# FNet and GEGLU layers on one core: the down projection of the last layer as seven block products that give y^T

## The chip, the cores and the metric

The kernel runs on one core of a Trainium2 chip. TensorE (PE) multiplies, VectorE (DVE) and ScalarE (ACT) work elementwise, GpSimd (POOL) and SyncE (SP) issue DMAs here; POOL also computes a few one-column values. The metric is the device time of one execution in microseconds (us). Three runs of the kernel before gave 1659.72, 1661.08 and 1661.01, median 1661.01.

## The reference

Four layers alternate, each as x + layer(layernorm(x)), all in float32. x is 2048 tokens by D = 512, F = 1792.

```
def _A_ref(x, dft_seq_re, dft_seq_im, dft_hid_re, dft_hid_im):
    a = jnp.einsum("bsd,ed->bse", x, dft_hid_re)
    b = jnp.einsum("bsd,ed->bse", x, dft_hid_im)
    return jnp.einsum("ts,bse->bte", dft_seq_re, a) - jnp.einsum("ts,bse->bte", dft_seq_im, b)
def _B_ref(x, w_gate, w_up, w_down):
    return (_gelu(x @ w_gate) * (x @ w_up)) @ w_down

x = x + _A_ref(_layernorm(x), ...)   # layer 0
x = x + _B_ref(_layernorm(x), ...)   # layer 1
x = x + _A_ref(_layernorm(x), ...)   # layer 2
x = x + _B_ref(_layernorm(x), ...)   # layer 3
```

## The kernel before

**Precision.** Every float32 operand of a product is split into two float32r tiles: ScalarE copies it to hi (line 126), VectorE computes lo = x - hi (line 127). A product of two split operands is three matmuls, hi by hi, hi by lo, lo by hi: `mm3`, lines 160 to 162. Each has a 128x128 stationary operand and a 128x512 moving one.

**Storage.** All working tiles of 128x512 come from `sb`, a list of NSLOT = 98 slots of SBUF that are taken from the front of a free list and put back at its end; accumulators come from `ps8`, the eight banks of PSUM. During part of a mix layer the tile `wide` (four slots' size) is lent to the list (`lend`, `reclaim`). The program is written in the Tile framework, which orders each engine's instructions at build time by a model of their readiness, so the order of the calls is a priority and not the order of execution.

**Mix layers (0 and 2).** The sequence DFT and the hidden DFT; the first is already done with seven block products instead of eight (Strassen-Winograd): `a11`, `a12`, `s2`, `s4` run over blocks b of 512 tokens, `hid_groups` follows.

**GEGLU layers (1 and 3).** `geglu(w, layer)` handles 1024 tokens at a time, w = 0 and 1, as two parts of 512 tokens. For n from 0 to 13 `up(n)` computes 256 columns' worth of gate (n even) or up (n odd) products, also as seven block products (S2, S1, A11 of n+1, S3, S4, A12 of n+1, A22; six matmuls each). ScalarE copies some of the sums out of PSUM (`copied`, line 155), VectorE adds others (line 151), ScalarE applies gelu (line 825), VectorE multiplies (line 839); the results are h[f, part], 128 columns of F by 512 tokens, transposed.

**The down projection before.** `down_steps(f, part)` takes the split w_down rows of f, already divided in DRAM (`wds`), and multiplies for each of four 128-token groups i: stationary is h[f, part] for these tokens, moving is w_down[f], 128x512; the sum over f = 0..13 gathers in `acc[part][i]`. `ready` splits h up to EARLY = 2 steps ahead. Eight steps of part 0 run between the products of `up` (from n = LAG = 6 on), the last six and the 14 of part 1 after the loop. `add_rows` adds x to the four sums (`x_add`, line 196) and POOL writes the rows (line 198). In the very last half, `last_downs` (TAIL = 4) orders the last four f by token group, so that each group of rows is added and written by SP while the next is multiplied.

**Queues.** `take` hands out operands in a fixed list, `items`; `load_next` issues their loads on SP (line 239) some items ahead (AHEAD, RAW, and NEAR for those that need no split, `whole`). Other work (norms, the blocks of the next half from `block_steps`, loads of divided gate and up weights by `piece_load`, line 815) is put into `queue`, and `step` runs one entry per product. `weight_steps(n)` loads gate and up weights in layer 1, forms S1 to S4, splits them and writes them to DRAM from POOL (lines 226 and 795). `terms_ahead`, `first_rows`, `second_rows` and `combine` prepare the next mix layer at the end of layer 1.

Of the kernel before, what the change touches and what calls it, by code (L numbers as in the profile page):

```python
# [14 lines left out]
P = 128  # L15
# [10 lines left out]
AHEAD = 5  # L26
RAW = 4
WARM = 16
LAG = 6
NEAR = 2  # L30
# [3 lines left out]
NSLOT = 98  # L34
FORE = {0: 4, 2: 2}
TAIL = 4
# [4 lines left out]
def fnet_geglu(ctx: ExitStack, tc: tile.TileContext, x_in, ws, wh, wgu, wdn, out):  # L41
# [33 lines left out]
    tpool = ctx.enter_context(tc.tile_pool(name="turned", bufs=1))  # L75
    slots = ctx.enter_context(tc.tile_pool(name="slots", bufs=1))
# [12 lines left out]
    class Slots:  # L89


        def __init__(self, pool, name, n):
            self.pool, self.name, self.free, self.held = pool, name, list(range(n)), {}
            self.least, self.lending = n, False
# [9 lines left out]
        def put(self, *tiles):  # L104
            for t in tiles:
                n = self.held.pop(id(t))[0]
                if isinstance(n, int) or self.lending:
                    self.free.append(n)

        def lend(self, tile):  # L110

            self.lending = True
            self.free = [(tile[:, i * 512:(i + 1) * 512],) for i in range(NT)] + self.free

        def reclaim(self):
            self.lending = False
            self.free = [n for n in self.free if isinstance(n, int)]
# [62 lines left out]
    def x_load(layer, i):  # L180
        t = sb.get()
        nc.sync.dma_start(t, rows(layer, i))
        return t
# [35 lines left out]
    wds = {f: dram.tile([P, 1024], F32, name=f"wd{f}") for f in range(NF)}  # L219

# [9 lines left out]
    stream = {"loaded": 0, "split": 0, "used": 0}  # L230
    raws, parts = {}, {}

    def load_next():
        n = stream["loaded"]
        dtype, addresses, _, _ = items[n]
        raws[n] = []
        for a in addresses:
            t = sb.get(dtype)
            stream["last"] = nc.sync.dma_start(t if dtype == F32 else f32(t), a)
            raws[n].append(t)  # L240
        stream["loaded"] += 1

    def split_next():
        n = stream["split"]
        while stream["loaded"] <= min(n + RAW, len(items) - 1):
            if stream["loaded"] > n + NEAR and items[stream["loaded"]][2] is whole:
                break
            load_next()
        parts[n] = items[n][2](*raws.pop(n))
        stream["split"] += 1  # L250

    def take():
        n = stream["used"]
        while stream["split"] <= min(n + AHEAD, len(items) - 1):
            need = items[stream["split"]][3]
            if need and need not in cs and stream["split"] > n:
                break
            if items[stream["split"]][2] is whole and stream["split"] > n + NEAR:
                break
            split_next()  # L260
        stream["used"] += 1
        return parts.pop(n)
# [93 lines left out]

    def mix_items(layer):
        def raw(make, *tiles):
            items.append((F32, tiles, make, None))

        for b, what in plan(layer):
            tiles = [[ws[(b * 2 + m) * NS + k] for k in range(NS)] for m in range(2)]
            (a11, a12), (a21, a22) = ((r[:NK], r[NK:]) for r in tiles)
            hold = b >= FORE[layer]
            if what == "A11":
                for k in range(NK):
                    raw(as_is if bare(layer, b, what) else make_a11(k) if hold else plain, a11[k])
            elif what == "A12":
                for t in a12:
                    raw(plain, t)  # L370
            elif what == "S2":
                for i, k in skewed(3):
                    if i == 0:
                        raw(make_s2(k), a21[k], a22[k], *(() if hold else (a11[k],)))
                    else:
                        raw(make_s1(k) if i == 1 else make_s3(k))
            elif what == "S4":
                for i, k in skewed(2):
                    if i == 0:
                        raw(make_s4(k), a12[k])  # L380
                    else:
                        raw(plain, a22[k])
            else:
                for m, c in what:
                    if layer == 0 and b == 0:
                        items.append((F32, (wh[m * ND + c],), make_hid_first(m, c), (m, c)))
                    else:
                        items.append((F32R, halves(whs[m, c]), make_hid(m, c), (m, c)))

    for layer in range(0, 4, 2):  # L390
        mix_items(layer)
        for w in range(NB // 2):
            for part in range(2):
                for f in range(NF):
                    if layer == w == part == 0:
                        items.append((F32, (wdn[f],), make_down_first(f), None))
                    else:
                        items.append((F32R, halves(wds[f]), whole, None))
# [87 lines left out]
    def second_rows(layer, k):  # L486
        second_norm(layer, k)
        second_parts(k)
# [32 lines left out]
    def block_steps(layer, w):  # L521
# [4 lines left out]
        def norm(i):  # L526

            def run():
# [5 lines left out]
                if n == 0:  # L534
                    assert all(isinstance(n, int) for n, _ in sb.held.values())
                    wide[part] = tpool.tile([P, NT * D], F32, name="wide")
# [66 lines left out]
    def mix(layer):  # L603
# [54 lines left out]
        def a12(b):  # L658
            side = [ps8.get() for _ in range(2)]
            for k in range(NK):  # L660
                six(side, "B21", k, k == 0, k == NK - 1)
# [17 lines left out]
        def s2(b):  # L679
            last, fore = b == NB - 1, b < FORE[layer]  # L680
            if b == 0:
                sb.lend(tpool.tile([P, NT * D], F32, name="wide"))
            if b == NB - 3:
                sb.reclaim()
# [77 lines left out]
    pieces = (("A11", "A12"), ("S2", "S3"), ("S1", "A22"), ("S4",))  # L762
# [4 lines left out]
    def weight_steps(n):  # L767
# [3 lines left out]
        def load():  # L771
# [4 lines left out]
            with tc.issue_after(stream["last"].ins):  # L776
                nc.sync.dma_start(src[0], wgu[n, :, :512])
                nc.sync.dma_start(v["A22"], wgu[n, :, 512:768])
                nc.sync.dma_start(v["A21"], wgu[n, :, 768:])
# [7 lines left out]
        def divide(i):  # L787
            def run():
                to = wblocks[n][:, i * 1024:min((i + 1) * 1024, 7 * 512)]
# [6 lines left out]
                piece_here(n, i, t)  # L796
# [3 lines left out]
        return load, [sums] + [divide(i) for i in range(len(pieces))]  # L800

# [26 lines left out]
    def geglu(w, layer):  # L828
# [71 lines left out]
        def up(n, down):  # L900
# [5 lines left out]
            u[n] = copied(chain[n])  # L906
            next(down, None)
# [35 lines left out]

        xrows = []
# [8 lines left out]
        def last_downs(tail):  # L953

            fs = range(NF - tail, NF)
            vs = [take() for _ in fs]
            for f in fs:
                ready(f, 1)
            for i in range(NT):
                ts = slice(i * P, (i + 1) * P)  # L960
                for f, v in zip(fs, vs):
                    hs = h[f, 1]
                    mm3(acc[1][i], (hs[0][:, ts], hs[1][:, ts]), v, f == 0, f == NF - 1)
                x_add(layer, (w * 2 + 1) * NT + i, xrows.pop(0), acc[1][i], engine=nc.sync)

        before_mix = w == 1 and layer < 3
        if before_mix:
            slow.extend((lambda k=k: terms_ahead(layer + 1, k, NK)) for k in range(NK))
        if w == 0:
            norms, others = block_steps(layer, 1)  # L970
            slow.extend(norms)
        first(0)
        second(0)
        for n in range(NF):
            up(n, down_steps(n - LAG, 0) if n >= LAG else iter(()))
        for bc in list(blocks):
            sb.put(*blocks.pop(bc))
        load_rows(0)
        if w == 0:
            while slow:  # L980
                slow.pop(0)()
            queue.extend(others)
        elif before_mix:
            queue.extend((lambda k=k: first_rows(layer + 1, k)) for k in range(NK))
            for k in range(NT):
                queue.append(lambda k=k: second_rows(layer + 1, k))
                queue.append(lambda k=k: combine(k))
            queue.extend((lambda k=k: combine_late(k)) for k in range(NT))
        for f in range(NF - LAG, NF):
            down(f, 0)  # L990
        add_rows(0)
        if w == 0:
            queue.extend((lambda n=n, i=i: piece_load(n, i)) for n in range(2) for i in range(len(pieces)))
        tail = TAIL if layer == 3 and w == 1 else 0
        for f in range(NF - tail):
            if f == NF - max(2, tail + 1):
                load_rows(1)
            down(f, 1)
            while len(queue) > 2 * (NF - 1 - f):
                step()  # L1000
        if tail:
            last_downs(tail)
        else:
            add_rows(1, before_mix)
        if before_mix:
            queue.extend((lambda k=k: second_rows(layer + 1, k)) for k in range(NT, NK))
            queue.extend((lambda k=k: combine(k)) for k in range(NT, NK))
            queue.extend((lambda k=k: combine_late(k)) for k in range(NT, NK))
# [85 lines left out]
```

## Time and profile before

| | |
|---|---|
| median of three runs | 1661.01 us |
| the profiled execution's own time | 1656.89 us |
| its span, first to last instruction | 1655.1 us |
| PE busy | 1637.7 us, 99% |
| DVE, ACT, POOL busy | 1027.5, 780.5, 188.9 us |
| granted TensorE clock, mean | 0.998 |
| moved by DMA | 399.99 MB |

Line numbers L... are those of the kernel before. A row of a group reads: line, engine, operation, out<-in by the program's names (s a slot, p a bank of PSUM), shapes, count, then busy time and mean duration of one, then how long the engine sat idle before them and what ended that. A row of stages reads: the stretch in us from the span's start, its length, then for each engine busy time and (number of instructions), the granted clock, the share of the 16 DMA engines' time and GB/s. Layer 3 starts at about 1233 us; its second half starts at about 1442 us.

### The profile page before, as it was taken

What the parts mean: (1) busy time and instruction counts of PE and PEld (TensorE: products, weight loads), DVE (VectorE), ACT (ScalarE), POOL (GpSimd) and SP (SyncE); (2) the same over time, 40 slices, a digit from 0 to 9 for tenths busy, and PEclk for the clock granted to TensorE, in tenths of its full rate; (3) what the DMA queues carried; (4) which work ended last, traced back from release to release, by engine and by line L of the source; (5) the groups of instructions that cost most, each with busy time, mean ns of one, the idle gap of its engine ahead of it and who ended that gap; (6) DMA issues with size and microseconds to landing.
All of it is one profiled execution on the core that took longest, in us unless ns stands there. A gap on an engine that the chain in (4) does not pass through costs nothing.

```text
span 1655.1 us, 22345 instructions
## 1 busy us (share of the span) xinstructions
PE 1637.7 (99%) x7168; PEld 1345.6 (81%) x7168; DVE 1027.5 (62%) x1756; ACT 780.5 (47%) x1496; POOL 188.9 (11%) x344
## 2 busy tenths in 40 slices
PE   9999998999999999999999999999999999999999
PEld 6878887877888888888878888888888888888887
DVE  8997777798776643334598776777944336233251
ACT  7743335545676524435584333664545435133330
POOL 3211001112544101000110000110010000000000
PEclk9999999999999999999999999999999999999999
DMA  9768677879976898566665767686798657956471
GB/s 364 235 217 278 209 241 250 288 274 321 355 271 240 284 367 275 174 183 213 233 216 185 221 210 230 206 269 227 214 340 296 198 164 243 374 171 191 148 240 51
DMA packets 218965, 399.99 MB, mean 242 GB/s; under 512 B 27232, under 2 KB 47200, under 8 KB 217824
## 3 DMA queue, kind: packets, MB, share of 16 engines
q1 hardware_dynamic: 200256, 333.02, 61.8%
q0 software_dynamic: 18592, 65.55, 10.5%
q8 instruction: 56, 0.92, 0.2%
q14 instruction: 61, 0.50, 0.1%
HBM read 331.87 MB, written 66.58 MB: 241 GB/s over the span
## 4 chain that ended last, share of the span: by engine, by line
PE 89%; DVE 4%; DMA 2%; ACT 2%; issue 1%; POOL 1%; SPq 0%; DVEq 0%; POOLq 0%; ACTq 0%
PE p L161 30%; PE p L160 29%; PE p L162 29%; DVE s L127 3%; DVE s L148 1%; DMA s<-x 1%; PE p L647 1%; ACT s L126 1%; DVE s L151 0%; ACT s L438 0%; DMA s<-ws 0%; DMA x<-s 0%; POOL rstd L432 0%; ACT s L440 0%; DMA s<-m_sum 0%
## 5 line engine op out<-in xcount | busy, mean ns | idle before, releaser
L161 PE MATMUL p<-s,s 128*128 128x512 f32 x2368 | 922.5, 390 | 6.9 <-DVE s L127 6.8
L162 PE MATMUL p<-s,s 128*128 128x512 f32 x2368 | 910.3, 390 | 0.0
L160 PE MATMUL p<-s,s 128*128 128x512 f32 x2368 | 902.0, 390 | 5.0 <-DVE s L151 3.9
L126 ACT ACTIVATE s<-s 128x512 fp32r<-128x512 f32 (+1 forms) x754 | 437.4, 616 | 448.2 <-DVE s L148 119.7
L127 DVE TENSOR_TENSOR s<-s,s 128x512 fp32r<-128x512 f32 (+1 forms) x754 | 484.8, 674 | 95.4 <-ACT s L126 62.4
L161 PEld LDWEIGHTS p<-s,s 128*128 128x128 f32 x2368 | 445.2, 188 | 103.7 <-DVE s L127 11.0
L160 PEld LDWEIGHTS p<-s,s 128*128 128x128 f32 x2368 | 445.0, 188 | 100.4 <-DVE s L151 3.6
L162 PEld LDWEIGHTS p<-s,s 128*128 128x128 f32 x2368 | 445.1, 188 | 93.7 <-DVE s L127 0.8
L151 DVE TENSOR_TENSOR s<-s,p 128x512 f32<-128x512 f32 x320 | 213.6, 683 | 349.1 <-PE p L162 283.9
L148 DVE TENSOR_TENSOR s<-s,s 128x512 f32<-128x512 f32 (+1 forms) x296 | 174.1, 604 | 50.3 <-DMA s<-ws 26.7
L155 ACT ACTIVATE s<-p 128x512 f32<-128x512 f32 x216 | 126.5, 592 | 151.6 <-PE p L162 148.7
L825 ACT ACTIVATE s<-s 128x512 f32<-128x512 f32 x112 | 70.4, 628 | 90.8 <-DVE s L151 89.6
L151 DVE TENSOR_TENSOR s<-s,s 128x512 f32<-128x512 f32 (+1 forms) x69 | 43.5, 633 | 51.8 <-DMA s<-ws 34.7
L198 POOL DMA_DIRECT2D x<-s x48 | 26.4, 551 | 357.0 <-DVE s L151 355.5
L441 POOL TENSOR_SCALAR rstd<-rstd 128x1 f32<-128x1 f32 x48 | 14.5, 301 | 455.4 <-ACT s L440 360.5
L438 ACT ACTIVATE s<-s 128x512 f32<-128x512 f32 x48 | 29.9, 623 | 65.7 <-DMA s<-x 53.8
L839 DVE TENSOR_TENSOR s<-s,s 128x512 f32<-128x512 f32 x84 | 57.8, 689 | 1.8
L226 POOL DMA_DIRECT2D wb<-s x84 | 45.8, 547 | 101.1 <-ACT s L126 69.6
L460 ACT ACTIVATE s<-s,shift,rstd 128x512 f32<-128x512 f32 x64 | 51.4, 808 | 9.8 <-DVE shift L433 6.0
L198 POOL DMA_DIRECT2D out<-s x12 | 6.5, 543 | 291.4 <-DVE s L151 288.4
L839 DVE TENSOR_TENSOR s<-s,p 128x512 f32<-128x512 f32 x28 | 19.2, 685 | 28.7 <-PE p L162 28.7
L440 ACT ACTIVATE s<-s,mean 128x512 f32<-128x512 f32 x48 | 34.3, 715 | 0.6
(47 smaller groups left out, 316.9 us busy)
## 6 DMA issues: line engine op xcount, KB each, us to landing
s<-ws SPq DMA_DIRECT2D x408, 256.0 KB, 4.1
s<-wb SPq DMA_DIRECT2D x294, 256.0 KB, 4.3
s<-wd SPq DMA_DIRECT2D x196, 256.0 KB, 4.7
s<-wh SPq DMA_DIRECT2D x118, 256.0 KB, 4.6
s<-x SPq DMA_DIRECT2D x102, 256.0 KB, 4.7
wb<-s POOLq DMA_DIRECT2D x98, 256.0 KB, 4.3
x<-s POOLq DMA_DIRECT2D x48, 256.0 KB, 4.7
s<-x SPq DMA_DIRECT2D x128, 64.0 KB, 3.4
```

The source lines that it names most:

```text
L126: nc.scalar.activation(hi, src, AF.Copy)
L127: nc.vector.tensor_tensor(lo, src, f32(hi), op=ALU.subtract)
L148: nc.vector.tensor_tensor(out, a, b, op=ALU.subtract)
L151: nc.vector.tensor_tensor(out, a, b, op=ALU.add)
L155: nc.scalar.activation(v, src, AF.Copy)
L160: nc.tensor.matmul(ps, ah, bh, start=start, stop=False, skip_group_check=True)
L161: nc.tensor.matmul(ps, ah, bl, start=False, stop=False, skip_group_check=True)
L162: nc.tensor.matmul(ps, al, bh, start=False, stop=stop, skip_group_check=True)
L226: nc.gpsimd.dma_start(a, f32(t))
L460: nc.scalar.activation(z, x, AF.Identity, bias=shift, scale=rstd)
L825: nc.scalar.activation(t, g, AF.Gelu_apprx_tanh)
L839: nc.vector.tensor_tensor(t, t, v, op=ALU.mult)
```

## The change

In layer 3, both halves (`SEVEN`), the products with w_down are computed transposed and by blocks. A pair k of F blocks (k = 0..6) and the two token parts make h a 2x2 block matrix; w_down's rows of the pair and the two halves of D make the other. Seven products per k, each with the weights' 128x128 pieces as the stationary operand and a combination of h (128x512) as the moving one, for two column groups c; six matmuls a product. The sums are y^T, 128 columns of D by 512 tokens. VectorE turns these in 32x32 blocks and adds them to a tile of x that was loaded in the same arrangement (`load_turned`, pieces of 512 bytes); four DMAs from POOL write it back.

- 13 of the products of a half run in `up` (`beside`): A11 of k at n = 2k+1, A12 of k at n = 2k+2; the other 36 follow in the order `DOWN_LATE`.
- `pair_combined`, `second_made`, `fourth_made` form the combinations of h; `prepared` splits them up to two products ahead, A11 and A12 at once where they are used.
- The seven weight blocks of each k are made once, in layer 1, by `weight_steps` on a second array `wdc`: the load of k = 0 and 1 and the division of k = 0 at the end of half 0, the rest during `up` of half 1.
- `last_downs` is gone.
- NSLOT is 94; the new tile `xwide` takes the four slots' room and is lent to the list from the first `s2` until layer 3.
- `whole` items are loaded up to 3 ahead (NEAR[0]) instead of 2, and 2 or 6 ahead for the new products. (MORE, `order` and its use in `a12` act only if layer 1's second half is in `SEVEN`; it is not.)
- `second_rows` loads rows that are not in SBUF from POOL's queue, no longer from SP's; in layer 1's second half they are put into the queue after the adds of part 0.

```diff
-NEAR = 2
+NEAR = 3, 2, 6
-NSLOT = 98
+NSLOT = 94
+SEVEN = (3, 0), (3, 1)
-TAIL = 4
+MADE = 4
+LEAD = 3
...
+    NP = NF // 2
+    DOWN_UP = [(name, k) for k in range(NP) for name in ("A11", "A12")]
+    DOWN_LATE = [("S1", k) for k in range(LEAD)] + [DOWN_UP.pop()]
+    DOWN_LATE += [p for k in range(NP) for p in [("S2", k)] + [("S1", k + LEAD)] * (k + LEAD < NP)]
+    DOWN_LATE += [("S4", k) for k in range(2)]
+    for k in range(2, NP):
+        DOWN_LATE += [("S3", 3 * (k - 2) // 2 + i) for i in range(1 + k % 2) if 3 * (k - 2) // 2 + i < NP] + [("S4", k)]
+    DOWN_LATE += [("A22", k) for k in range(NP)]
...
     def second_rows(layer, k):
+        if NK + k not in fresh:
+            fresh[NK + k] = x_load(layer, NK + k, nc.gpsimd)
...
             product(n, chain[n], "S2", "T2", False, True)
             u[n] = copied(chain[n])
+            down = beside(n)
             next(down, None)
             side[n] = ps8.get()
             product(n, side[n], "S1", "T1", True, True)
...
+        def pair_combined(k):
+            b11, b12, b21, b22 = h4[k] = [h.pop((2 * k + i, part)) for i in range(2) for part in range(2)]
+            minus(b11, b12, b11)
+            minus(b12, b22, b12)
+            bs["A12", k] = split_slot(b21)
+            if k < MADE:
+                second_made(k)
+                fourth_made(k)
...
+        def down_product(name, k):
...
+            t, = take()
+            parts = bs.pop((name, k))
+            for c in range(2):
+                hi, lo = (t[:, h][:, c * P:(c + 1) * P] for h in half)
+                mm3(banks[bank][c], (hi, lo), parts, name in ("A11", "A12", "S1") and k == 0, k == NP - 1)
+                yield
...
+        def ended(name, ps):
+            if name in ("A11", "S1", "S2"):
+                ys[name] = [copied(p) for p in ps]
+            elif name == "A22":
+                for c in range(2):
+                    turned_rows(0, 2 + c, ps[c])
+                    ps8.put(ps[c])
+                rows_done(0)
+            else:
+                to = ys.pop({"A12": "A11", "S3": "S1", "S4": "S2"}[name])
+                for c in range(2):
+                    plus(to[c], to[c], ps[c])
...
+                for c in range(2):
+                    turned_rows(name != "A12", 2 * (name == "S3") + c, to[c])
...
+        def beside(n):
+            if plain_down:
+                return down_steps(n - LAG, 0) if n >= LAG else iter(())
+            k = (n - 1) // 2
+            if n % 2:
+                bs["A11", k] = split_slot(h[2 * k, 0])
+                return down_product("A11", k)
+            if n:
+                pair_combined(k)
+                return down_product("A12", k)
+            return iter(())
...
+        def turned_rows(part, c, src):
+            t = sb.get()
+            blocks_of = "p (j e) -> p j e"
+            nc.vector.transpose(t.rearrange(blocks_of, e=32), src.rearrange(blocks_of, e=32))
+            to = xturned[part].rearrange("p (j c e) -> p j c e", c=NT, e=32)[:, :, c]
+            plus(to, to, t.rearrange(blocks_of, e=32))
+            sb.put(t)
+
+        def rows_done(part):
+            rows_moved(layer + 1, part, lambda v, outside: nc.gpsimd.dma_start(outside, v))
...
+            for i, (name, k) in enumerate(late):
+                for more in late[i:i + EARLY + 1]:
+                    prepared(*more)
+                for _ in down_product(name, k):
+                    pass
+                step()
...
+                if i == len(late) // 3:
+                    load_turned(1)
```

More of the change, by code (lines that the diff above doesn't have):

```diff
@@ L534, in run @@
                 if n == 0:
-                    assert all(isinstance(n, int) for n, _ in sb.held.values())
+                    assert not sb.out("z")
                     wide[part] = tpool.tile([P, NT * D], F32, name="wide")
@@ new lines, in geglu @@
+        BANKS = {"A11": "chain", "S2": "chain", "S3": "chain", "A22": "chain", "A12": "two", "S1": "side", "S4": "side"}
+        def down_product(name, k):
+            bank = BANKS[name]
+            if bank not in banks:
+                banks[bank] = [ps8.get() for _ in range(2)]
+            t, = take()
[4 more added lines that the diff above has]
+                yield
+            sb.put(t, *parts)
+            if k == NP - 1:
+                ended(name, banks[bank])
@@ L951, in add_rows @@
                 x_add(layer, (w * 2 + part) * NT + i, xrows.pop(0), acc[part][i], keep)
[L953 to L964, printed above, removed]
         before_mix = w == 1 and layer < 3
+        plain_down = (layer, w) not in SEVEN
         if before_mix:
@@ L971, in geglu @@
             slow.extend(norms)
+        if not plain_down and layer == 1 or layer == 3:
+            sb.reclaim("x")
         first(0)
```

221 lines of the change are left out of this document (157 added, 64 removed).

## The prediction

> **What bounds the kernel now.** I read the page first, for which engine is full, then the stages by stretches of time, then PE's waits, then the last microseconds.
>
> ```profile
> span 1655.1 us, 22345 instructions
> PE 1637.7 (99%) x7168; PEld 1345.6 (81%) x7168; DVE 1027.5 (62%) x1756; ACT 780.5 (47%) x1496; POOL 188.9 (11%) x344
> ```
> ```profile
> 579.00:633.00 54.00, 54.00 (x240) 44.72 (x239) 23.60 (x39) 15.19 (x31) 5.89 (x12) 1.00 1.01 365
> 633.00:788.00 155.00, 155.00 (x685) 128.34 (x685) 57.33 (x89) 71.97 (x142) 4.78 (x12) 1.00 0.63 201
> 1388.00:1442.00 54.00, 54.00 (x240) 44.72 (x239) 23.99 (x39) 13.81 (x23) 2.18 (x4) 1.00 0.96 345
> 1442.00:1597.00 155.00, 155.00 (x685) 128.34 (x685) 58.66 (x88) 57.17 (x95) 2.15 (x4) 1.00 0.61 191
> 1442.00:1651.20 209.20, 209.20 (x923) 172.88 (x922) 71.52 (x108) 62.16 (x103) 4.32 (x8) 1.00 0.52 166
> ```
> ```profile
> PE p L161 <- DVE s L127: 6.8, 7, 2.7
> PE p L160 <- DVE s L151: 3.9, 2, 2.7
> PE p L160 <- ACT s L126: 1.0, 2, 0.8
> ```
>
> PE is busy in every microsecond of layer 3, at a granted clock of 1.00; the three waits, 11.7 us in all, lie ahead of it. A busy PE need not be a PE at its peak, so I take its pace: 209.20 us for 923 matmuls is 0.2266 us each. VectorE works 72 of these 209 us, ScalarE 62. So a matmul less in layer 3 is worth 0.2266 us, as long as PE still never waits there. At the end the last matmul is followed by one add, one write and its landing (below).
>
> **The saving.** Before, a half's down projection is 14 f x 2 parts x 4 groups x 3 = 336 matmuls. After, it is 7 products x 7 pairs x 2 column groups x 3 = 294, of the same shapes (stationary 128x128, moving 128x512). That is 42 less per half, 84 in layer 3: 84 x 0.2266 = **19.0 us off**.
>
> **The end of the kernel.** Before:
>
> ```profile
> 1650.81 0.39 PE L162 MATMUL p<-s,s 128*128 128x512 f32 x1
> 1651.24 0.69 DVE L151 TENSOR_TENSOR s<-s,p 128x512 f32<-128x512 f32 x1 [2.03 <-PE p L162]
> 1643.79 8.49 SPq L198 DMA_DIRECT2D out<-s  x4
> ```
> ```profile
> L538 DVE STREAM_TRANSPOSE wide<-s 128x512 f32<-128x512 f32 x32 | 22.5, 706 | 12.9 <-ACT s L460 12.4 <-DMA wb<-s 0.4
> L198 POOL DMA_DIRECT2D x<-s x48 | 26.4, 551 | 357.0 <-DVE s L151 355.5
> ```
> ```profile
> x<-s POOLq DMA_DIRECT2D x48, 256.0 KB, 4.7
> s<-t SPq DMA_DIRECT2D x128, 64.0 KB, 2.7
> out<-s POOLq DMA_DIRECT2D x12, 256.0 KB, 4.8
> out<-s SPq DMA_DIRECT2D x4, 256.0 KB, 2.0
> ```
>
> Call the start of the last matmul L. Its add starts at L + 0.43, ends at L + 1.12, the last SP issue ends at 1643.79 + 8.49 = 1652.28 = L + 1.47, and the span ends at L + 4.3. After, the last product (A22, k = 6) ends two sums, the first three matmuls (0.68) ahead of the second. VectorE turns and adds the first, then the second: start at L - 0.68 + 0.43, then 0.71 + 0.69 twice, end at L + 2.55, which is 1.4 later. All four writes need both sums, since each carries 32 partitions of every column group; POOL issues them one after the other, 4 x 0.55 = 2.2 instead of one SP issue of 0.33: 1.9 later. The landing: alone at the end SP's took 2.0; POOL's rows stand at 4.7 and 4.8, but amid traffic. The pieces are 512 bytes now, as in s<-t, where 64 KB took 2.7. The difference is between 0 and 2.8; I take 1.4, halfway, since both a new queue and smaller pieces speak for more and the quiet end for less. **Sum 1.4 + 1.9 + 1.4 = 4.7 us on**; bounds 3.3 and 6.1. A gain is excluded: four dependent operations and four issues replace one and one. In the first half (1442) the same writes end behind the next half's products, as `add_rows`' four do now, and cost nothing; without that cover it would be the same 4.7.
>
> [...]
>
> **The elementwise work in layer 3.** The prices:
>
> ```profile
> L127 DVE TENSOR_TENSOR s<-s,s 128x512 fp32r<-128x512 f32 x724 | 473.5, 685 | 87.9 <-ACT s L126 55.9 <-PE p L161 12.2 <-PE p L162 6.3
> L126 ACT ACTIVATE s<-s 128x512 fp32r<-128x512 f32 x724 | 426.5, 624 | 443.8 <-DVE s L148 118.3 <-PE p L162 87.3 <-PE p L161 76.3
> L151 DVE TENSOR_TENSOR s<-s,p 128x512 f32<-128x512 f32 x320 | 213.6, 683 | 349.1 <-PE p L162 283.9 <-ACT s L155 59.3 <-DMA s<-wd 3.0
> L148 DVE TENSOR_TENSOR s<-s,s 128x512 f32<-128x512 f32 x206 | 138.9, 685 | 32.0 <-DMA s<-ws 26.7 <-DMA s<-t 1.9 <-PE p L161 1.8
> L155 ACT ACTIVATE s<-p 128x512 f32<-128x512 f32 x216 | 126.5, 592 | 151.6 <-PE p L162 148.7 <-PE p L161 1.3
> ```
> ```profile
> 1410.43 3.69 DVE L127 TENSOR_TENSOR s<-s,s 128x512 fp32r<-128x512 f32 x6
> 1417.09 1.29 DVE L127 TENSOR_TENSOR s<-s,s 128x512 fp32r<-128x512 f32 x2 [2.97 <-PE p L161]
> ```
>
> Per half VectorE does 49 splits for 28, 28 differences of h that are new, 6 sums and 8 turns and 8 adds for 8 adds: 21 + 28 + 6 + 8 = 63 more operations of about 0.69, some 43 us. The second half has 209 - 72 = 137 idle: no bound there. ScalarE gets 21 copies to hi (0.62) and 6 out of PSUM (0.59), 17 us, with more idle still.
>
> The tight place is the stage after the loop of the first half, 36 products or 216 matmuls, 48.9 us. What VectorE must do there: 36 splits, 8 differences, 22 for outputs, and the next half's blocks, 14 splits and 8 differences: 88 operations. Back to back six take 3.69, 0.615 each: 54 us; at 0.688 each 60.5. So 5 to 12 us too much, if none ran earlier. But the stage of today shows that work does run early: PE multiplies until 1442, and VectorE is through with its splits at 1418, having done 39 operations in the stretch where by the calls 14 + 8 for the blocks, 20 splits of h and 8 adds, 50 in all, belong. The loop before it has 155 - 62 us idle VectorE. How much of the new work can run ahead is limited by free slots, which the trace does not count: cost between 0 and 11.7; I take 1.5, near the row that shows PE waiting for nothing at today's stage. In the second half no blocks follow, 66 operations or 41 to 45 us stand against 48.9: 0.
>
> **In the loop** 13 products per half use operands that are split right where they are called. Called in this order: S2, ScalarE's copy of its sum, the split for A11 or A12, its matmuls, S1. If ScalarE ran in that order, PE would wait for one copy and one hi, 0.59 + 0.62 = 1.2 us, each time. But the order is settled at build time, and the trace shows PE off the call order:
>
> ```profile
> 1303.11 0.39 PE L161 MATMUL p<-s,s 128*128 128x512 f32 x1
> 1303.33 0.39 PE L160 MATMUL p<-s,s 128*128 128x512 f32 x1
> 1304.47 0.62 PE L162 MATMUL p<-s,s 128*128 128x512 f32 x2
> ```
>
> Behind a product's second matmul (L161) comes another's first (L160), and the L162 that was passed over stands 1.1 us later. So S1 can go ahead of a late A11. What stays is the model's error: between 0 and 1.2 x 26 = 31 us, I take 1.0.
>
> **Layers 0 to 2.** Making the weights costs per k four adds of 128x256, three splits and one half split, loads of 512 KB and writes of 1.8 MB. Five k fall into 633 to 788, where VectorE and ScalarE are busy 57 and 72 of 155; 5 x 2.36 MB in 155 us is 76 GB/s on top of 201, below the 365 that the stage at 579 carries with PE full: 0. In that stage itself the DMA share is 1.01; k = 0 and the load of k = 1 bring 2.9 MB, 7.8 us of it. But it is prefetching, since the stretch behind it falls to 0.63 with PE full, so 0, bound 7.8. The four loads that move to POOL stand in its queue behind the writes of the same rows; behind them wait rstd values for the next norms, and for those PE at 842. The whole queue is 8.26 us busy of the last 54 of layer 1:
>
> ```profile
> 788.00:842.00 54.00, 54.00 (x240) 44.72 (x239) 35.89 (x67) 33.21 (x75) 8.26 (x15) 1.00 0.65 209
> 842.00:870.00 28.00, 26.40 (x116) 21.43 (x116) 23.91 (x46) 25.26 (x56) 5.16 (x11) 1.00 0.76 248
> ```
>
> PE loses 1.6 us in the 28 behind; a write's landing of 4.7 more or less could halve or treble that: -1 to +4, I take 0. Four slots fewer until the first `s2` in layer 0 shorten the prefetch by about two operands, 0 to 3 us, I take 0.5. Edits to NEAR: 0, as loads run as far ahead as today or further.
>
> **Sum.** 1655.1 - 19.0 + 4.7 + 1.5 + 1.0 + 0.5 = 1643.8 of span. The profiled execution took 1.8 more than its span (1656.9), and the median 4.1 more than that: 1643.8 + 5.9 = 1649.7, so **1650**.
>
> **Rivals.**
>
> *Nothing is lost but the end.* All elementwise work runs ahead; the end costs its lower bound: 1661 - 19.0 + 3.3 = 1645. For it: PE's unbroken 209 us; against: 36 products in a row each with a fresh split.
>
> *VectorE becomes the bound after the loop of the first half.* No slots are free to split early, and PE waits the upper bound, 11.7 us, where I took 1.5: 1649.7 + 10.2 = 1660, hardly a change. For it: 88 operations against 48.9 us; against: the splits that run 24 us ahead today.
>
> *The fixed order bites: slower.* Place: the 26 products in the loops. If the build keeps ScalarE's copy of S2 ahead of the hi, or models VectorE too fast, PE waits 1.2 each time: 31 us, 1661 - 19.0 + 4.7 + 31 = 1678. It decides above (19.0 - 4.7)/26 = 0.55 us each; below that the change still gains. Against: the passed-over L162, and that no wait is seen in `up` today; for: today's down products there work on h that is six steps old, the new ones on h that is one step old. [...]
>
> *The seven products are not what runs* (matmuls not fewer) I leave out: the loops fix the count.
>
> **Numbers.** Forecast 0.63 (own range 1646 to 1655), nothing lost 0.15, VectorE bound 0.12, fixed order 0.10. A measurement here can tell about 0.2%, 3.3 us, from no change. Faster takes the first two and the better half of the third (below 1657.7): 0.85; same 0.05; slower 0.10. The range, 1643 to 1661, holds the forecast, both neighbours and the bounds of end and stage; the slower rival stays outside.
>
> **What would show it.** PE has 84 matmuls fewer, and layer 3 runs some 400 instead of 418 us. The last matmul is followed by about 9.0 us instead of 4.3, with turn and add twice and four POOL writes of 512-byte pieces. In the stretch behind the first half's loop VectorE is over 85% busy; PE waits for L127 there, if at all. In the loops PE's waits for ScalarE or VectorE sum to about 1 us; if they reach 14, I am wrong, and over 1 us per product the slower rival is right.

## The result, and the profile after

| | before | after |
|---|---|---|
| median of five runs | 1659.72 us | 1652.49 us |
| lowest to highest | 1658.94 to 1661.08 | 1649.72 to 1654.09 |
| the profiled execution's own time | 1656.89 us | 1651.61 us |
| its span | 1655.1 us | 1649.5 us |

The ratio is 0.9952 with a 95% interval of 0.9938 to 0.9967: 7.2 us faster by the medians, where 11 were forecast and 19 are in the matmuls alone. The time lies inside the forecast range, on the slow side of the likeliest case. Ratios are of fast executions alone, and the one profiled execution of the run f1_two_queues below was a slow one (2742.46 us at a granted clock of 0.556), so its trace is not read. Lines L... of the runs below are those of each kernel's own file; the roles are named.

The page of the changed kernel, then its stages: layer 3's first loop and the stage behind it, the second loop and the stage behind it, and what follows the last matmul. The columns are those of the rows of before.

```profile
span 1649.5 us, 22669 instructions
PE 1620.7 (98%) x7084; PEld 1330.9 (81%) x7084; DVE 1130.6 (69%) x1938; ACT 822.9 (50%) x1578; POOL 220.1 (13%) x401
```
```profile
1236.00:1387.00 151.00, 151.00 (x668) 125.08 (x667) 77.72 (x121) 72.42 (x138) 7.09 (x16) 1.00 0.74 221
1387.00:1436.00 49.00, 48.90 (x214) 39.84 (x214) 47.21 (x78) 27.70 (x49) 0.00 (x0) 1.00 0.86 280
1436.00:1587.00 151.00, 151.00 (x667) 125.07 (x667) 74.92 (x114) 57.28 (x99) 5.19 (x8) 1.00 0.69 208
1587.00:1636.30 49.30, 49.30 (x218) 40.56 (x216) 33.85 (x56) 16.33 (x29) 2.57 (x4) 1.00 0.37 104
1636.30:1649.50 13.20, 0.05 (x1) 0.00 (x0) 1.98 (x4) 0.00 (x0) 2.57 (x4) 0.58 0.53 124
```

PE has 84 matmuls fewer and is full through both halves of layer 3 but for 0.1 us, although VectorE is 96% busy behind the first half's loop. So nearly the whole 19.0 us are taken there. The last row is where about half of them go: 13.2 us in which PE does nothing.

Behind the last matmul, in order of time: the last matmul, the turns, the adds, the writes.

```profile
1635.71 1.40 DVE L1120 STREAM_TRANSPOSE s<-p 128x512 f32<-128x512 f32 x2 [3.54 <-PE p L174]
1635.96 0.39 PE L174 MATMUL p<-s,s 128*128 128x512 f32 x1
1637.03 1.25 DVE L163 TENSOR_TENSOR xwide<-xwide,s 128x512 f32<-128x512 f32 x2
1638.57 2.57 POOL L1126 DMA_DIRECT2D out<-xwide  x4 [3.54 <-DVE xwide L163]
```

From the start of the last matmul to the end of the span it is now 1649.5 - 1635.96 = 13.5 us, before 4.3. The adds end at +2.3 (before +1.1), the last issue at 1641.14, +5.2 (before +1.5), and then 8.4 us pass (before 2.8). The next rows are the landing of these four writes, POOL's queue entries of the end of the program (minimum, median and maximum duration in ns, first and last start), two stages of the end, and the last 1.5 us of before:

```profile
out<-xwide POOLq DMA_DIRECT2D x4, 256.0 KB, 4.7
```
```profile
L1292 POOLq DRAIN  x3: 40/102/8583, 1640.1 to 1649.2; - x3
```
```profile
1641.50:1645.50 4.00, 0.00 (x0) 0.00 (x0) 0.00 (x0) 0.00 (x0) 0.00 (x0) 0.50 0.79 193
1645.40:1649.50 4.10, 0.00 (x0) 0.00 (x0) 0.00 (x0) 0.00 (x0) 0.00 (x0) 0.50 0.00 0
```
```profile
1653.62:1655.12 1.50, 0.00 (x0) 0.00 (x0) 0.00 (x0) 0.00 (x0) 0.00 (x0) 0.58 0.00 0
```

In the last 4.1 us no DMA engine moves anything (share 0.00), yet the kernel has not ended: POOL's queue is in an entry called DRAIN, of 8.6 us. Before, 1.5 us lay between the last bytes and the end. The transfers are one part of the new end, POOL is another.

The last matmul itself starts 14.85 us earlier than before, not 19.0, so 4.2 us went elsewhere, most of them ahead of layer 3. PE's waits, first those of before that weren't shown, then all of after, then of after from 842 to 1236 us (layer 2):

```profile
PE p L1014 <- POOL ident masks.py:199: 1.4, 1, 1.4
PE p L647 <- ACT s L460: 0.2, 1, 0.2
```
```profile
PE p L173 <- DVE s L139: 6.9, 5, 1.8
PE p L172 <- DVE s L163: 4.3, 3, 2.1
PE p L172 <- ACT s L138: 2.3, 3, 0.9
PE p L1211 <- POOL ident masks.py:199: 1.4, 1, 1.4
PE p L172 <- DVE xwide L163: 0.3, 1, 0.3
PE p L172 <- DVE wide L163: 0.2, 1, 0.2
```
```profile
PE p L173 <- DVE s L139: 2.6, 2, 1.5
PE p L172 <- DVE s L163: 1.8, 1, 1.8
PE p L172 <- ACT s L138: 1.3, 2, 0.7
PE p L172 <- DVE xwide L163: 0.3, 1, 0.3
PE p L172 <- DVE wide L163: 0.2, 1, 0.2
```

The sums are 13.3 before and 15.4 after, 2 of the 4.2 us. Within them layer 0 waits less (8.7 for 11.7) and layer 2 more (6.2 for 1.6). The waits are not all: the matmuls that run in the same three stretches of both kernels (to 424 us about layer 0, to 842 layer 1, to 1236 layer 2) tell more. First before, then after:

```profile
0.00:424.00 424.00, 412.21 (x1765) 331.94 (x1766) 346.40 (x633) 215.80 (x403) 68.40 (x109) 0.99 0.80 270
424.00:842.00 418.00, 418.00 (x1846) 346.12 (x1845) 227.79 (x398) 223.57 (x457) 83.30 (x159) 1.00 0.75 254
842.00:1236.00 394.00, 392.30 (x1729) 324.10 (x1729) 296.69 (x488) 195.21 (x380) 25.77 (x53) 1.00 0.71 232
```
```profile
0.00:424.00 424.00, 415.22 (x1791) 337.27 (x1792) 352.15 (x644) 223.15 (x414) 72.36 (x120) 1.00 0.82 278
424.00:842.00 418.00, 417.45 (x1840) 344.83 (x1839) 250.03 (x444) 234.93 (x485) 106.89 (x203) 1.00 0.81 287
842.00:1236.00 394.00, 387.74 (x1694) 318.27 (x1694) 292.74 (x482) 191.07 (x368) 23.48 (x47) 1.00 0.70 228
```

At 0.2266 us each, PE gained 26 matmuls or 5.9 us in layer 0, lost 6 or 1.4 us in layer 1 and 35 or 7.9 us in layer 2: 3.4 us in all, and the other 0.8 of the 4.2 are left for layer 3. So layer 2 lost 7.9 us where its waits grew by 4.6, and layer 0 hid most of it.

### The profile page after: what moved, and what is told of

The parts are those of the page before. It is cut to its first block, busy times and chain, and to the rows that moved or that the text cites. A ratio compares the mean times of both kernels' runs of the same rounds, so it can differ in the third digit from the quotient of the medians.

```text
span 1649.5 us, 22669 instructions
## 1 busy us (share of the span) xinstructions
PE 1620.7 (98%) x7084; PEld 1330.9 (81%) x7084; DVE 1130.6 (69%) x1938; ACT 822.9 (50%) x1578; POOL 220.1 (13%) x401
## 4 chain that ended last, share of the span: by engine, by line
PE 74%; issue 12%; DMA 5%; DVE 5%; ACT 2%; POOL 0%; SPq 0%; POOLq 0%; DVEq 0%; ACTq 0%
PE p L173 24%; PE p L174 24%; PE p L172 24%; DVE s L139 3%; DMA s<-ws 2%; DVE s L160 1%; DMA xwide<-ws 1%; PE p L695 1%; ACT s L138 1%; DVE s L163 1%; DMA s<-wgu 1%; DMA wide<-x 1%; DMA wide<-ws 1%; DVE xwide L160 0%; PE p L1211 0%
## 5 line engine op out<-in xcount | busy, mean ns | idle before, releaser
L173 PE MATMUL p<-s,s 128*128 128x512 f32 x2340 | 911.8, 390 | 7.0 <-DVE s L139 6.9
L174 PE MATMUL p<-s,s 128*128 128x512 f32 x2340 | 901.6, 390 | 0.0
L172 PE MATMUL p<-s,s 128*128 128x512 f32 x2340 | 883.1, 391 | 7.3 <-DVE s L163 4.3
L138 ACT ACTIVATE s<-s 128x512 fp32r<-128x512 f32 (+1 forms) x709 | 414.8, 615 | 395.3 <-DVE s L160 100.0
L139 DVE TENSOR_TENSOR s<-s,s 128x512 fp32r<-128x512 f32 (+1 forms) x709 | 457.9, 672 | 98.6 <-ACT s L138 78.3
L172 PEld LDWEIGHTS p<-s,s 128*128 128x128 f32 x2340 | 439.7, 188 | 104.3 <-DVE s L163 5.6
L173 PEld LDWEIGHTS p<-s,s 128*128 128x128 f32 x2340 | 440.2, 188 | 101.1 <-DVE s L139 9.5
L174 PEld LDWEIGHTS p<-s,s 128*128 128x128 f32 x2340 | 440.1, 188 | 92.4 <-DVE s L139 0.9
L163 DVE TENSOR_TENSOR s<-s,p 128x512 f32<-128x512 f32 x266 | 178.2, 682 | 186.2 <-PE p L174 96.4
L160 DVE TENSOR_TENSOR s<-s,s 128x512 f32<-128x512 f32 (+1 forms) x273 | 161.6, 604 | 24.8 <-DMA s<-ws 16.2
L138 ACT ACTIVATE s<-xwide 128x512 fp32r<-128x512 f32 (+1 forms) x119 | 72.6, 619 | 74.9 <-PE p L173 21.3
L884 ACT ACTIVATE s<-s 128x512 f32<-128x512 f32 x97 | 60.8, 629 | 94.2 <-DVE s L163 91.9
L139 DVE TENSOR_TENSOR s<-xwide,s 128x512 fp32r<-128x512 f32 (+1 forms) x119 | 79.9, 678 | 17.2 <-ACT s L138 13.5
L163 DVE TENSOR_TENSOR s<-s,s 128x512 f32<-128x512 f32 (+1 forms) x54 | 33.0, 612 | 34.2 <-DMA s<-ws 19.9
L898 DVE TENSOR_TENSOR s<-s,s 128x512 f32<-128x512 f32 x71 | 48.9, 688 | 1.5
L506 ACT ACTIVATE s<-s,shift,rstd 128x512 f32<-128x512 f32 x54 | 43.6, 809 | 11.7 <-DVE shift L479 5.3
L484 ACT ACTIVATE s<-s 128x512 f32<-128x512 f32 x39 | 24.3, 624 | 39.8 <-DMA s<-x 36.2
```

The source lines that it names most:

```text
L138: nc.scalar.activation(hi, src, AF.Copy)
L139: nc.vector.tensor_tensor(lo, src, f32(hi), op=ALU.subtract)
L160: nc.vector.tensor_tensor(out, a, b, op=ALU.subtract)
L163: nc.vector.tensor_tensor(out, a, b, op=ALU.add)
L172: nc.tensor.matmul(ps, ah, bh, start=start, stop=False, skip_group_check=True)
L173: nc.tensor.matmul(ps, ah, bl, start=False, stop=False, skip_group_check=True)
```

## The experiments

Open after the comparison: what makes the end long (POOL, the pieces, the amount); whether layer 2's waits come from the change and from which part; whether VectorE was close to being the bound. My theory: the end is POOL's issues and drain; the 94 slots cost in layers 0 to 2; VectorE is just short of being the bound. The table gives for each kernel the ratio to before, PE's waits ahead of layer 3, those of layer 2 among them (both from the rows of waits of a profiled execution, added up), and the us from the start of the last matmul to the end of the span.

| run | ratio (95% interval) | waits | of layer 2 | end |
|---|---|---|---|---|
| before | 1 | 13.3 | 1.6 | 4.3 |
| after | 0.9952 (0.9938 to 0.9967) | 15.3 | 6.2 | 13.5 |
| e1_sp_end | 0.9928 (0.9908 to 0.9948) | 19.8 | 5.4 | 10.4 |
| e2_one_half | 0.9953 (0.9935 to 0.9970) | 17.2 | 5.8 | 4.2 |
| e3_no_seven | 1.0048 (1.0031 to 1.0065) | 17.8 | 5.7 | 4.3 |
| e4_no_seven_slots98 | 1.0008 (0.9999 to 1.0018) | 14.9 | 2.2 | 4.2 |
| e5_no_seven_no_weights | 0.9994 (0.9984 to 1.0004) | 14.6 | 2.3 | 4.1 |
| e6_busy | 0.9963 (0.9944 to 0.9981) | 16.1 | 6.0 | 13.5 |
| e7_three | 1.0133 (1.0114 to 1.0152) | 42.8 | 22.0 | 10.3 |
| e9_sp_load | 0.9950 (0.9937 to 0.9964) | 15.9 | 5.1 | 13.3 |
| f1_two_queues | 0.9943 (0.9929 to 0.9958) | not read | not read | not read |
| f3_lent_first | 1.0086 (1.0071 to 1.0101) | 33.5 | 14.2 | 10.4 |
| f4_not_lent | 1.0025 (1.0015 to 1.0035) | 23.8 | 6.1 | 10.3 |
| g1_long_pieces | 0.9937 (0.9920 to 0.9953) | 14.9 | 6.4 | 9.7 |

After, e1 and g1 differ by their edits in nothing ahead of the end, and their waits read 15.3, 19.8 and 14.9: one execution's sum is good to some 5 us. What layer 2 shows is steadier. In the seven kernels that keep the change's list, its weights and its layer 1 (after, e1, e2, e3, e6, e9, g1) its waits are 5.1 to 6.4 us, and 1694 to 1704 matmuls run from 842 to 1236 us, 25 to 35 fewer than the 1729 of before, which is 5.7 to 7.9 us. Layer 0 is not steady: 1761 to 1791 matmuls in the same kernels, 1765 before, so its gain in the profiled execution of after can't be put down to the change.

**The last writes from SP.**

```diff
+            engine = nc.sync if layer == 3 and w == 1 else nc.gpsimd
-            rows_moved(layer + 1, part, lambda v, outside: nc.gpsimd.dma_start(outside, v))
+            rows_moved(layer + 1, part, lambda v, outside: engine.dma_start(outside, v))
```

> The last half's eight writes of turned rows are issued by SP instead of POOL; nothing else. After the change 13.5 us lie between the start of the last matmul and the end of the span (before: 4.3), and POOL's queue shows one drain of 8.6 us at the end. Theory: POOL is what ends last, by its four issues of 0.65 and by the drain behind them; then SP's four issues of about 0.35 and a landing of about 5 leave 9 to 10 us behind the last matmul and the kernel gets 3.5 to 4.5 us faster than the changed one, ratio to before about 0.993. Rival: the transfers in 512-byte pieces are what takes long; then only the issue time is saved, about 1.3 us, and 12 us stay behind the last matmul.

The last four issues on SP, the landing of these writes there, and the last 1.5 us:

```profile
1642.86 0.39 PE L174 MATMUL p<-s,s 128*128 128x512 f32 x1
1645.20 3.39 SPq L1127 DMA_DIRECT2D out<-xwide  x4
```
```profile
out<-xwide SPq DMA_DIRECT2D x4, 256.0 KB, 4.4
```
```profile
1651.75:1653.25 1.50, 0.00 (x0) 0.00 (x0) 0.00 (x0) 0.00 (x0) 0.00 (x0) 0.50 0.00 0
```

1653.3 - 1642.86 = 10.4 us instead of 13.5: 3.1 saved, and with the last issue no earlier behind the last matmul (+5.7 here, +5.2 with POOL). The last bytes have moved 8.9 us behind the start of the last matmul (1651.75), with POOL 9.4 (1645.40); from there to the end it is 1.5 us, as before the change, and with POOL 4.1. So 2.6 of the 3.1 are POOL's drain and 0.5 the transfers; the issues gave nothing. SP's took 0.85 on average (0.3 to 1.4), not the 0.35 of my expectation, and a landing of 4.4 still follows, for 4.7 with POOL. The theory holds for the drain; not for the rest.

**Two queues for the last writes.**

```diff
+            last = layer == 3 and w == 1
+            engines = [nc.sync, nc.scalar] * 2 if last else [nc.gpsimd] * NT
-            rows_moved(layer + 1, part, lambda v, outside: nc.gpsimd.dma_start(outside, v))
+            rows_moved(layer + 1, part, lambda v, outside: engines.pop(0).dma_start(outside, v))
```

> The changed kernel with the last half's writes issued by SP and ScalarE's queue in turn, two each per part. With SP alone the four issues of 512-byte pieces took 3.4 us and 10.4 us lay behind the last matmul. Theory (the issue and POOL's drain were what was left to save): 8.5 to 9.5 us behind the last matmul, 4 to 5 less than in the changed kernel, ratio to before 0.991 to 0.993. Rival (the transfers bound the end now): still 10 us or more.

The ratio, 0.9943, is that of the changed kernel within its interval, above the 0.991 to 0.993 of the theory. The end was read in f4_not_lent, which ends the same way:

```profile
1650.49 0.39 PE L174 MATMUL p<-s,s 128*128 128x512 f32 x1
1652.84 0.85 SPq L1126 DMA_DIRECT2D out<-xwide  x2
1652.84 0.93 ACTq L1126 DMA_DIRECT2D out<-xwide  x2
```
```profile
out<-xwide SPq DMA_DIRECT2D x2, 256.0 KB, 4.9
out<-xwide ACTq DMA_DIRECT2D x2, 256.0 KB, 5.4
```
```profile
1659.30:1660.80 1.50, 0.00 (x0) 0.00 (x0) 0.00 (x0) 0.00 (x0) 0.00 (x0) 0.50 0.00 0
```

All four are issued by 1653.77, 3.3 us behind the last matmul instead of 5.7, but the span ends 10.3 behind it, as with SP alone (10.4): the last bytes have moved 8.8 us behind it, at 1659.30, with SP alone 8.9. The rival is right: once POOL's drain is gone, the transfers bound the end.

**Pieces of 8 KB in place of 512 bytes.** As the run before, but each turned tile's partitions are written one behind the other.

```diff
...
+            if last:
+                flat = xs[layer + 1, w * 2 + part].rearrange("(q r) d -> q (r d)", r=NT)
+                for p in range(NT):
+                    cut = slice(p * 32, (p + 1) * 32)
+                    engines.pop(0).dma_start(flat[cut], xturned[part][cut])
+                return
...
```

> f1_two_queues, with the last half's turned tiles written in pieces of 8 KB (a partition's 2048 values one behind the other) instead of 512 bytes, so these 1024 rows of the output are not in their places. Theory (what is left of the end, 10.3 us behind the last matmul with SP and ScalarE issuing, is mostly the pieces): 7 to 8 us behind the last matmul, 2 to 3 us faster than f1_two_queues. Rival (1 MB and its landing take that long in any pieces): still about 10 us.

```profile
1636.83 0.39 PE L174 MATMUL p<-s,s 128*128 128x512 f32 x1
1639.17 0.78 SPq L1132 DMA_DIRECT2D out<-xwide  x2
```
```profile
out<-xwide SPq DMA_DIRECT2D x2, 256.0 KB, 4.4
```

1646.5 - 1636.83 = 9.7 us, 0.6 less than f4, where the theory had 2 to 3. The pieces are a small part of it at most. What is left is that 1 MB in four writes waits for the last add, where before one write of 256 KB did, which landed in 2.0. That each of the four reads 32 partitions, where that one read 128, is a rival that no run tests.

**One half only.** SEVEN holds (3, 0) alone; the last half is as before, its `last_downs` restored.

```diff
-SEVEN = (3, 0), (3, 1)
+SEVEN = ((3, 0),)
```

> Only the first half of layer 3 is done with seven products; the second half is done as before, with its last four f ordered by token group and written by SP. Theory (the loss is at the end of the kernel, and the second half itself runs at full PE pace): 42 matmuls come back, +9.5 us, and the end goes from 13.5 back to 4.3, -9.2, so the time is that of the changed kernel within 1 us, ratio to before about 0.995 to 0.996. Rival (the second half also loses PE time somewhere): faster than the changed kernel by more than 1.5 us.

0.9953 against 0.9952, the end 4.2. The theory holds as far as intervals of some 3 us can tell: 42 matmuls more, 9.5 us, and the old end, 9.3 less, cancel. The seven products of the second half gain nothing in this kernel that could be told.

**More work for VectorE in the first half.** Three turns for each, with the same result.

```diff
-            nc.vector.transpose(t.rearrange(blocks_of, e=32), src.rearrange(blocks_of, e=32))
+            for _ in range(3 if w == 0 else 1):
+                nc.vector.transpose(t.rearrange(blocks_of, e=32), src.rearrange(blocks_of, e=32))
```

> The changed kernel with each turn of the first half of layer 3 done three times over (the same result): 16 more VectorE operations of 0.6 to 0.7 us, 10 to 11 us, in or near the stage behind that half's loop, where VectorE is busy 47 of 49 us. Theory (VectorE is just short of being the bound there): PE waits 7 to 10 us more in layer 3, ratio to before about 1.000. Rival (the build's order runs work ahead and puts the rest behind the next half's products): less than 2 us more than the changed kernel, ratio 0.995 to 0.9965.

```profile
1387.00:1436.00 49.00, 48.39 (x212) 39.44 (x211) 46.64 (x77) 27.19 (x48) 0.00 (x0) 1.00 0.83 271
1436.00:1587.00 151.00, 151.00 (x667) 125.01 (x667) 83.58 (x131) 57.14 (x99) 5.19 (x8) 1.00 0.71 209
```

My theory falls. The stage behind the loop is as full as without them (46.64 for 47.21), the next loop has 83.58 for 74.92, 8.7 more, and PE waits 0.6 us in all of layer 3, for a load of weights and not for VectorE:

```profile
PE p L172 <- DMA s<-wc: 0.6, 2, 0.4
```

The extra work slid behind the next half's products. VectorE's 96% in that stage is a full queue of work, not a bound here.

**Everything but the seven products.** SEVEN is empty, `last_downs` restored; the second weights are made and not used.

```diff
-SEVEN = (3, 0), (3, 1)
+SEVEN = ()
```

> Everything of the change but the seven products: both halves of layer 3 as before, with the old end; the second set of weights is still made in layer 1 (and not used), the list has 94 slots plus the lent tile, prefetch 3, the four loads from POOL. Theory (layers 0 to 2 pay for the change through the order that the build chooses): PE's waits ahead of layer 3 are about 15 us as in the changed kernel, against 12 before, and the time is 1 to 4 us above before, ratio 1.001 to 1.0025. Rival (layers 0 to 2 pay nothing, the differences there are chance): waits of about 12 us, ratio 1.000.

0.5% slower than before, more than I expected. The waits ahead of layer 3 are 17.8, and layer 3 now waits for w_down's loads:

```profile
PE p L173 <- DMA s<-wd: 2.0, 1, 2.0
```

**The same with 98 slots.** As the last, and without lending the x tile:

```diff
-NSLOT = 94
+NSLOT = 98
...
-                if "x" not in sb.lent:
-                    sb.lend(upool.tile([P, NT * D], F32, name="xwide"), "x")
```

> As the kernel without the seven products (e3_no_seven), but with 98 slots and no lent x tile, as before the change; weights still made, prefetch 3, loads from POOL. PE's waits in layer 2 were 1.6 us before the change and 5.4 to 6.2 in the five kernels with 94 slots. Theory (the slots: four fewer that can hold a split operand): waits in layer 2 fall to about 2 us, the waits for w_down loads in layer 3 vanish, and the time is back at that of before, ratio about 1.000. Rival (prefetch, making the weights or the loads from POOL): waits in layer 2 stay at 5 to 6 us, ratio above 1.003.

1.0008, layer 2 waits 2.2 (1723 matmuls in its stretch, 1697 in e3), and no wait for w_down: as the theory said. With the second weights made, the four slots that the x tile takes are what makes the rest of the change cost half a per cent.

**The same with 94 slots, and without making the weights.**

```diff
-            if layer == 1 and w == 1:
+            if False:
                 k, odd = divmod(n + 3, 2)
...
-            if layer == 1:
+            if False:
                 down_making.update((k, down_weight_steps(k)) for k in range(2))
```

> As e3_no_seven, but the second set of weights isn't made (nothing reads it there). Theory (the slots cost): layer 2's waits stay at 5 to 6 us, layer 1's shrink to under 1, ratio 1.003 to 1.005. Rival (making the weights costs): waits ahead of layer 3 as before, ratio about 1.000.

0.9994, layer 2 waits 2.3 (1716 matmuls): the rival's ratio. Neither the slots alone nor the weights alone cost anything that can be told by the ratio; both together do. How they reach layer 2 is not shown: the weights take slots while they are made, out of a list that is four shorter, but the changed kernel writes the last of them at 739.8 us, 100 us before layer 2 begins.

**The four loads from SP.**

```diff
-            fresh[NK + k] = x_load(layer, NK + k, nc.gpsimd)
+            fresh[NK + k] = x_load(layer, NK + k)
```

> The changed kernel with the four loads of x before layer 2 issued by SP again. Theory (the slots cost in layer 2, not these loads): waits of 5 to 6 us in layer 2 as in the changed kernel, ratio 0.994 to 0.997. Rival (the queue of the four loads costs): waits of about 2 us in layer 2, ratio about 0.992.

0.9950, layer 2 waits 5.1: no effect, as the theory said.

**Other ways to share the slots.** Both as f1_two_queues; in the first a plain tile takes a lent piece where one is free, in the second the x tile is never lent.

```diff
+            if dtype == F32:
+                at = next((i for i, n in enumerate(self.free) if not isinstance(n, int)), at)
```

> f1_two_queues, and a request for a plain float32 tile takes a lent piece first if one is free, so that the 94 own slots, the only ones that can hold split operands, stay free for those. Theory (slots for split operands are what is short in layers 0 to 2): PE's waits in layer 2 fall from 5 to 6 us to 2 to 3, 3 us faster than f1_two_queues. Rival (the waits come from how the build happens to order the work, not from a lack of slots): they change in either direction without this, somewhere in layers 0 to 2, sum within 3 us of that of the changed kernel (16 us ahead of layer 3).

```diff
-                if "x" not in sb.lent:
-                    sb.lend(upool.tile([P, NT * D], F32, name="xwide"), "x")
```

> f1_two_queues without lending the x tile at all: 94 slots in layers 0 to 2 instead of 94 and 4. Theory (slots are short there): waits ahead of layer 3 grow by 3 us or more over f1_two_queues. Rival (the order by chance): within 3 us, in either direction.

PE's longest waits in f3_lent_first, in layer 1 and in layer 2, and then the longest of f4_not_lent in layer 2:

```profile
PE p L174 <- DMA s<-wd: 6.3, 1, 6.3
```
```profile
PE p L174 <- ACT s L140: 13.9, 3, 8.3
```
```profile
PE p L172 <- ACT s L138: 3.3, 2, 3.1
```

Without the lent tile the waits are 23.8 against some 15 to 20, and the ratio is 1.0025 where f1 has 0.9943: the four lent slots do help. But giving the lent pieces out first, which should have kept slots free for split operands, made 33.5 of it and 1.0086: worse by far than either expectation. So it is not the count of slots for split operands alone; a slot taken anew early makes its next load wait for its last reader, and which slot comes next sets the order of the build. Both steps are argued, not shown.

**Seven products in layer 1 too**, with the last writes from SP.

```diff
-SEVEN = (3, 0), (3, 1)
+SEVEN = (1, 1), (3, 0), (3, 1)
```

> Seven products in the second half of layer 1 too (SEVEN with (1, 1), with what the code has ready for that case), and the last half's rows written by SP. Theory: 42 matmuls less, 9.5 us, the end 3 us shorter than in the changed kernel, but the stage before layer 2 now has VectorE work for both; it was 60 of 82 us busy there before: gain of 8 to 12 us over the changed kernel, ratio 0.988 to 0.991. Rival (VectorE becomes the bound at the boundary to layer 2, where PE waited already): gain under 4 us, ratio above 0.9925, waits of over 10 us near 840.

The first stretch of layer 2, and PE's longest wait in layer 2:

```profile
870.00:960.00 90.00, 78.62 (x296) 60.72 (x297) 77.11 (x139) 53.20 (x107) 5.06 (x12) 0.88 0.44 145
```
```profile
PE p L172 <- ACT s L138: 14.7, 3, 9.2
```

1.0133: 42 matmuls fewer and, by the medians (1681.45 and 1652.49), 29 us slower than the changed kernel. PE waits 22.0 us in layer 2, where VectorE and ScalarE prepare the mix, and its clock falls to 0.88 there; 8.6 us more are waits in layer 1, 3.4 of them for a load of weights. The rival is right on the place and the loss, not shown on the engine: 14.7 of the 22.0 us are put down to ScalarE's copies and 7.3 to VectorE, and VectorE is busy 77 of the 90 us. MORE and `order` act in this run too, so it is not a test of the seven products alone. What it shows is that a change that costs PE next to nothing in layer 3 is a loss at a boundary where PE waits for these engines.

No run is a version that clearly beats the changed kernel. Its last writes on SP save 3.1 us in the trace; the ratios, 0.9928 and 0.9943, overlap that of the changed kernel.

## Why the prediction was right, and which terms were off

- **The saving** of 84 x 0.2266 = 19.0 us: right but for some tenths: PE idles 0.1 us in layer 3, and 0.8 are lost there in all.
- **The end**, +4.7 with bounds of 3.3 and 6.1: wrong, +9.2. The turns and adds came as worked out (+1.2 for 1.4); the last issue came 3.7 later for 3.3; what follows it, for which I took 1.4 more, was 5.5 more. This is the step that was mis-sized, and two things were missing in it. I took the landing of one write of 256 KB where four are in flight: the last bytes have moved 4.3 us behind the last issue, before 1.3. And POOL's queue has a drain that lasts 2.6 us longer behind the last bytes than the end with SP does (e1). The 512-byte pieces that I weighed are some 0.6 (g1). The four writes took 6.8 us from the first issue (1638.57) to the last bytes (1645.40).
- **The stage behind the first half's loop**, 1.5 of 0 to 11.7: 0.1. The argument that work runs ahead or slides behind was right, and e6 shows how far: 16 operations more made PE wait for VectorE not at all in layer 3. The rival of the VectorE bound is refuted.
- **The loops**, 1.0 of 0 to 31: 0. PE never waits in them in the profiled execution, so the slower rival falls. That the build's order bridges the short distance is argued, and what would follow a wrong order no run shows. In seven other runs with these products (e1, e2, e6, e7, e9, f4, g1) PE waits 0.5 to 1.7 us in layer 3 for a load of the new weights, a wait that the prediction did not name.
- **Layers 0 to 2**, 0.5 in all: 3.4 by the matmuls of the profiled executions, made of 7.9 lost in layer 2, 1.4 in layer 1 and 5.9 gained in layer 0, which is not steady; and 8 us in e3 by the ratio, with the waits for w_down. This is the other term that was mis-sized. I priced the slots by the prefetch of layer 0 and the weights by VectorE's idle time, each by itself, and each alone is indeed free by the ratio (e4, e5); their joint effect in layer 2 I did not see, and its way there stays open. The move of four loads to POOL, 0 of -1 to +4, was right (e9).
- **The sum** of the span was 1643.8 and it is 1649.5, 5.7 more: the end took 4.5 more, the layers ahead of layer 3 took 2.9 more, loops and stage 1.7 less. The median is only 2.5 above the forecast, because I added the 4.1 us by which the median of before lay above its profiled execution, and after it is 0.9. That part of the closeness is luck, and so is layer 0's gain.

## What to carry to other kernels

Price the end of a kernel by what is still in flight behind the last add, all of it, and by the queue that carries it: the kernel ended 2.8 us behind the issue of one write from SP, and 8.4 behind the last of four from POOL. VectorE was 96% busy in a stage and still no bound, because its work could move (e6): repeat some of an engine's work and see whether anybody waits. Count the matmuls of each stage beside the waits: layer 2 lost 7.9 us where its waits grew by 4.6. And two edits that were each free alone by the ratio (1.0008 and 0.9994) cost half a per cent together (1.0048); test them together.

## What the hardware showed beside this

Idle time of the same length cost differently. In both kernels PE idles about 1.6 us at the start of layer 2, before in one wait, after in two of 1.1 and 0.6. Before, its clock stayed at 1.00 in the 28 us around it (row in the prediction); after, it did not:

```profile
842.00:870.00 28.00, 26.35 (x107) 20.86 (x107) 24.38 (x45) 22.69 (x45) 4.65 (x8) 0.94 0.75 239
```

With the same 26.4 us busy that is 107 matmuls instead of 116, 2 us lost again, and part of what layer 2 lost beyond its waits. In the same 28 us e9 idles 2.1 us at a clock of 0.94 and e4 1.0 us at 1.00. So idle time of some 1.6 us went with a lower clock in one execution and not in another. Whether this is why each kernel's runs spread by some us is not shown.
